# Moving the conversion of the channel weights to a later place in a planned order, with other places set anew

## The chip, the cores and the metric

The kernel runs on one core of a Trainium2 chip. The core has five engines that work beside each other, each through its own instructions in order: TensorE (PE) multiplies matrices, VectorE (DVE) and GpSimd (POOL) work elementwise, ScalarE (ACT) computes functions and copies, and SyncE (SP) issues the transfers between the memory and the core. They wait for each other through semaphores. The metric is the time of one execution in microseconds on the device.

## The reference

A hashed attention feeds a mixing layer. For 4 batches, 8 heads, 768 positions and 64 values per head:

```python
bits = (q @ proj > 0), (k @ proj > 0)            # 6 bits make a bucket
scores = (q @ k.T) / 8, -1e9 where the buckets of query and key differ
x = softmax(scores) @ v                          # heads side by side: (4, 768, 512)
theta = x @ w_theta
y = w_tok_r @ (x * cos(theta)) + w_tok_i @ (x * sin(theta))
u = x + y
out = u + relu(u @ w_ch)
```

w_theta and w_ch are 512 x 512, w_tok_r and w_tok_i 768 x 768; they arrive as 64-bit floats.

## The kernel before

**The work.** Attention goes by batch and pair of heads. For a pair, q and k are loaded and transposed (line 592), split into a high and a low part (597, 600), their sign bits computed (pb, 626), and the operands qt and kt put together by transfers on the SP queue (672 to 681). The maxima of the rows are taken from scores sq (723) and put into qt as a row (747). Then, for chunks of 512 columns, the scores st are multiplied, ACT takes the exponential pf (801) and its half-precision part p (807), POOL the rest of it (813), and PE sums po. norm (862) writes a head's columns of x. V has its own preparation (448 to 525).

The mixing of a batch (function moe) follows when its attention is done, and so runs beside the attention of the next batch. It takes theta for six tiles of 128 positions (transposed 907, hi and lo 912 and 916, product ps_th, then n 948 and the remainder 951), sine and cosine for two groups of three tiles (973, 974), then for each tile and each of the two parts f (985) and its two halves z (990, 996), the token sums py, u (1024), the channel product ps_r with wch, the end (1031) and the store (1034).

**The weights.** Each is turned from 64-bit floats to a high and a low part on the chip, once, before its first use. `widened` (349) loads the raw words on SP (358), builds the 32-bit magnitude with two DVE steps (366, 370), takes the sign and the magnitude on ACT (375, 376) and multiplies them on POOL or DVE (379, 382, 383). `split_weight` (389) adds the high part on ACT (394) and the low part on POOL or DVE (397). w_theta comes in four pieces of 128 x 512, w_ch in eight of 128 x 256. `prep_wtok` (402) does the token weights in T = 6 pieces, and transposes them on PE (424 to 428).

**The order.** Nothing of it is written out. Every operation has a due place, in units of attention: a batch is 24 units, a head 3. Batch b's mixing has G = 24 (b + 1). `issue_all` first walks the list by due place and gives the users of each buffer pool their ranks. Then it plays through the engines with estimated durations: whenever one is free, it takes, of the operations whose inputs are ready, the one due first for which buffers are there, so that an operation may run far ahead of its place where an engine would idle. Two things limit that. A buffer may be taken out of rank only within a window: less than 3 places past the first rank not yet served for the pools m and tmp, otherwise 1. And an operation is held back when one due over 2 units (AHEAD) earlier would become ready within 0.3 of its duration (HOLD). The sequence found is the program: on the chip each engine keeps it.

**The pools that matter here.** tmp has 3 buffers in SBUF; n (948), f (985) with its halves, and both buffers of a w_ch piece (the raw words and the floats) come from it. z0 and z1 have one each; the mixing's z lie in them, and the token weights and w_theta are built in them before. x has 2, for the attention's result, and the raw words of the token weights and of w_theta. m is 4 PSUM banks, for transposes, bits, po, py, theta and channel products.

**The due places.** Places of w_ch are WC + WCS (c + half / 2), lines 1093 and 1094. The token weights stand at W0 + WS tau (1043), w_theta at WTH + WTS c. For batch 0 theta of tile tt has 24 + 0.82 tt, the f of a group 24 + 0.82 (t1 - 0.5), where t1 is 3 and 6, and the token sum of tile t and what follows from it 24 + 8.904 + 2.702 t, with the sums themselves spread over the 6.16 units ahead of that. `at` (302) looks for a value of its own for a batch (TH0_3) and else takes the general one (TH0).

Of the kernel before, what the change touches and what calls it, by code (L numbers as in the profile page):

```python
# [31 lines left out]
def lsh_attention_moe_kernel(ctx: ExitStack, tc: tile.TileContext, q, k, v, proj, w_theta, w_tok_r, w_tok_i, w_ch, aff, out):  # L32
    nc = tc.nc
    PE, ACT, DVE, POOL = nc.tensor, nc.scalar, nc.vector, nc.gpsimd

    B, H, S, D = q.shape
# [17 lines left out]
    def bank(sl, shape, nm):  # L54
        return psum[sl.pool].tile(shape, F32, tag=sl.tag, bufs=1, name=nm)
# [52 lines left out]
    def op(name, prio, alts, deps=(), slots=(), table=None):  # L108
        return Op(name, prio, alts, deps, slots, table)

    def issue_all():
        left = {}
        rng = random.Random(SEED)
        for i, o in enumerate(ops):
# [63 lines left out]
        def key(o, e):  # L178
            return o.key
# [28 lines left out]
        while todo:  # L208
            progress = False
            for e in START:  # L210
# [3 lines left out]
                for o in avail[e]:  # L214
                    k_ = key(o, e)
                    if best is not None and k_ >= best:
                        continue
                    end = now + (HOLD * o.alts[e][0] if e != "SP" else 0)
                    if any(x.at < end and key(x, e)[0] + AHEAD < k_[0] for x in soon[e]):
                        continue  # L220
# [78 lines left out]
    def on(e, dur, fn):  # L299
        return {e: (dur, fn)}  # L300

    def at(nm, b):
        return globals().get(f"{nm}_{b}", globals()[nm])

    def pick(g, rule, alts):
        for lo, hi, engines in rule:
            if lo <= g < hi:
                return {e: alts[e] for e in engines}
        return alts
# [34 lines left out]
    def pow2_scale(amax, inv, s):  # L344
        DVE.tensor_scalar(inv, amax, 1e-30, 2.0**-13, ALU.max, ALU.mult)
        DVE.tensor_scalar(inv.bitcast(U32), inv.bitcast(U32), MASK, None, ALU.bitwise_and)
        DVE.tensor_scalar(s.bitcast(U32), inv.bitcast(U32), MASK, None, ALU.bitwise_xor)
# [39 lines left out]
    wready = {"th": [], "ch": [], "tk": []}  # L387

    def split_weight(src, dst, c, cols, nm, tag, stage, prio, by=1.0):
        lo, n = cols  # L390
        k_ = n / DM
        t, g, sz = widened([src[c * P : (c + 1) * P, lo : lo + n].bitcast(U32)], n, f"{nm}{c}_{lo}", tag, prio, stage=stage, by=by)
        dh, dl = (d[:, c, lo : lo + n] for d in dst)
        h_ = op("wh", prio, on("ACT", 100 + 420 * k_, lambda: ACT.activation(dh, t["w"][:, 0], AF.Copy)), [g], [sz])

        def low(eng):
            return lambda: eng.tensor_tensor(dl, t["w"][:, 0], dh.bitcast(F32), ALU.subtract)

        wready[nm].append(h_)
        wready[nm].append(op("wl", prio, {"POOL": (130 + 1100 * k_, low(POOL)), "DVE": (65 + 535 * k_, low(DVE))}, [h_], [sz]))  # L400

    def prep_wtok(tau, prio):
        am = const.tile([P, 1], F32, name=f"wam_{tau}")
        def scale(t):
            t["s"] = ap_.tile([P, 1], F32, tag="scw", bufs=T, name=f"scw_{tau}")
            pow2_scale(am, sinv[:, tau : tau + 1], t["s"])

        t, g, sz = widened(
            [src.bitcast(U32).rearrange("(p t) s -> p t s", t=T)[:, tau, :] for src in (w_tok_r, w_tok_i)],
            S, f"t{tau}", f"z{tau % 2}", prio, am, scaled=scale,  # L410
        )
        cs = slice(tau * P, (tau + 1) * P)
        TC = 4
        for c0 in range(0, 2 * T, TC):
            def chunk(c0=c0):
                u = {}
                sm_ = Slot("m")
                hi, lo = (wtk_[i].rearrange("p r t s -> p (r t) s")[:, c0 : c0 + TC, cs] for i in range(2))

                def tr():  # L420
                    u["pt"] = bank(sm_, [P, TC, P], f"pwt_{tau}_{c0}")
                    for n in range(TC):
                        r, tt = divmod(c0 + n, T)
                        PE.transpose(u["pt"][:, n, :], t["w"][:, r].rearrange("p (c t) -> p t c", t=T)[:, tt], ident)

                d = op("wtr", prio, on("PE", 109 * TC, tr), [g], [sz, sm_])
                e = op("wth", prio, on("ACT", 55 + 106 * TC, lambda: ACT.activation(hi, u["pt"], AF.Copy)), [d], [sm_])
                wready["tk"].append(op("wtl", prio, on("DVE", 66 + 133.5 * TC, lambda: DVE.tensor_tensor(lo, u["pt"], hi, ALU.subtract)), [e], [sm_]))

            chunk()  # L430
# [6 lines left out]
    vready = {b: [] for b in range(B)}  # L437

    def prep_v(b, hp, prio):
# [86 lines left out]

        r = op("vload", prio + LV0, on("SP", [(450, 2 * S * D * 4)], load), slots=[svb])
        r = op("vamax", prio, on("DVE", 870, amax), [r], [svb])
# [136 lines left out]
    def assemble(j, n_, t, prio, free_after):  # L665
# [12 lines left out]
        def bits():  # L678
# [7 lines left out]
            op("assemble", prio, on("SP", [(1000, 4 * D * n)] * 2 + [(1000, 2 * hd * n)] * 4, parts), t["parts"] + free_after, [sh]),  # L686
            op("assbits", prio + AB, on("SP", [(780, NM * n)] * 2, bits), t["bits"] + free_after, [sr]),
        ]
# [8 lines left out]
    def maxima(h, n_, b, G, asm):  # L697
# [14 lines left out]
        for n, (parts, cs) in enumerate(units):  # L712
            def one(n=n, parts=parts, cs=cs):
# [10 lines left out]

                pr = G + at("MX0", b) + at("MX1", b) * n * T / len(units)
                a = op("qmax", pr, on("PE", 280, scores), asm, [sx])
# [26 lines left out]

        pr = G + at("MX0", b) + at("MX1", b) * T
        a = op("vboth", pr, on("DVE", 110, both), vs, [smc])
# [11 lines left out]
    def step(g, b, h, blk, mxt, vt, piece):  # L767
# [15 lines left out]
        for c in range(nc_):  # L783
            def chunk(c=c):
# [18 lines left out]
                def p1(e):  # L803
                    def go():
                        o_ = wide("p1", sp1, F16)
                        if e == "ACT":
                            ACT.activation(o_, u["pf"], AF.Copy)  # L807
                        else:
                            DVE.tensor_copy(o_, u["pf"])
                    return go  # L810

                def p2(eng):
                    return lambda: eng.tensor_tensor(wide("p2", sp2, F16), u["pf"], u["p1"], ALU.subtract)  # L813
# [20 lines left out]
                last[n_].append(a)  # L834
                i = op("pf", G + PF, on("ACT", 490, pf), [a], [ss, spf], table="exp")
                d = [done] if done else [mxt["ftd"]] + vt["ready"]
                f = [sft] if c == 0 else []
                if vt["full"]:
                    return op("pv4", G + KV, on("PE", 900 + 29 * ni * (c == 0), pv), d + [i], [spf, sm_, vt["slot"], sx] + f)
                k1 = op("p1", G + KA, pick(g, P1, {"ACT": (525, p1("ACT")), "DVE": (337, p1("DVE"))}), [i], [spf, sp1])  # L840
                k2 = op("p2", G + KB, pick(g, P2, {"DVE": (610, p2(DVE)), "POOL": (1090, p2(POOL))}), [k1], [spf, sp1, sp2])
                return op("pv", G + KV, on("PE", 385 + 29 * ni * (c == 0), pv), d + [k1, k2], [sp1, sp2, sm_, vt["slot"], sx] + f)

# [19 lines left out]

        r = op("recip", g + KN, on("DVE", 90, recip), [done], [sm_])
        n = op("norm", g + KN, on("DVE", 135 + 67 * n_, norm), [r], [sm_, sx])
        for i in range(*piece):
# [3 lines left out]
    def moe(b, G):  # L870
        sx = xslot[b]
        sz = [Slot("z0"), Slot("z1")]
        t = {}
# [8 lines left out]
            t["z"] = {(r, i): zt[r][:, :, i] for r in range(2) for i in range(2)}  # L882
            t["zw"] = [zt[r].bitcast(F32).rearrange("p t i d -> p t (i d)") for r in range(2)]

        st0 = op("moe", G, on("DVE", 800, start), wready["tk"] + vready[b], sz)

        cnt = [0]
        tail = TAIL
# [151 lines left out]
    for b in range(B):  # L1040
        xready[b] = [[] for _ in range(NQ)]
    for tau in range(T):
        prep_wtok(tau, W0 + WS * tau)
    for c in range(NC):
        split_weight(w_theta, wth, c, (0, DM), "th", "z0", "x", WTH + WTS * c, 1.0 / TWO_PI)
        for half in range(2):
            split_weight(w_ch, wch, c, (half * DM // 2, DM // 2), "ch", "tmp", "tmp", WC + WCS * (c + 0.5 * half))
    g = 0
    for b in range(B):
        phase = str(b)  # L1050
        for hp in range(NP):
            t = prep_qk(b, hp, g, g)
# [3 lines left out]
            for j in range(2):  # L1056
                n = ((b * NP + hp) * 2 + j) % SETS
                free_after, last[n] = last[n], []
                G = g + sum(BLOCKS[k_][1] // 2 for _, k_ in order[: order.index((j, 0))])
# [5 lines left out]
    for b in range(B):  # L1065
        phase = str(b)
        moe(b, (b + 1) * H * NQ)
# [11 lines left out]
TAIL = ["m", "s"]  # L1079
ORDERS = [[(0, 0), (0, 1), (1, 0), (1, 1)], [(0, 0), (1, 0), (0, 1), (1, 1)]]  # L1080
WIN = {"m": 3, "tmp": 3}
MX0 = -3.0
MX1 = 0.377
PIECES = [{1: (0, 3)}, {0: (0, 2), 1: (2, 3)}]
PF = 0.11
KA = 0.3
KB = 0.629
KV = 0.573
KN = 1.022
AB = 0.145  # L1090
WTH = 16.607
WTS = 1.0
WC = 19.051
WCS = 0.722
P1 = [(0, 999, ["ACT"])]
P2 = [(0, 999, ["POOL"])]
# [1 line left out]
GR1 = 0  # L1098
GROUPS = [[(0, 3), (3, 6)], [(0, 4), (4, 6)], [(0, 2), (2, 4), (4, 6)]]
JIT = 0  # L1100
SEED = 0
TH0_3 = -1.231
TH1_3 = 0.851
Y0_3 = 9.278
# [1 line left out]
Y1_3 = 2.611  # L1106
MX0_0 = -3.0
MX1_0 = 0.377
AS0_0 = -4.85
PV0_0 = -4.074  # L1110
QK0_0 = -6.0
QK1_0 = -5.94
HOLD = 0.3
AHEAD = 2.0
QKL = -8.933
QK0 = -6.006
QK1 = -5.0
AS0 = -2.867
PV0 = -4.114
LV0 = -4.543  # L1120
W0 = 0.4
WS = 3.097
TH0 = 0.0
# [47 lines left out]
```

## Time and profile before

| what | value |
|---|---|
| median of 3 timed runs | 867.27 us (866.17 to 867.66) |
| the profiled execution | 863.75 us |
| its span, from the first to the last instruction | 862.0 us |
| mean granted clock of TensorE | 0.978 |
| instructions of the matrix products with w_ch | from 273.0 us on |
| conversion of w_ch, first to last instruction | 14.5 to 179.9 us |
| conversion of w_theta, first to last instruction | 132.8 to 184.1 us |

Times inside a profile count from the start of its span. An engine's busy time is the time in which it executes; a PE that is shown busy may still run at a lower clock, which stands beside it as the granted clock (1.00 is full speed). The durations that the prediction uses come from this one profiled execution; the timed runs are others, without the profiler.

### The profile page before, as it was taken

The page shows a single profiled execution, that of the slowest core. Times are in us where ns is not written, and L with a number is a line of the kernel's source. Part 1 is how long each engine was busy: PE and PEld are TensorE (multiplying, and loading weights), DVE is VectorE, ACT ScalarE, POOL GpSimd, SP SyncE. Part 2 cuts the span into 40 slices and gives each one's busy share as a digit, 9 for nine tenths or more (in the row PEclk, how much of TensorE's full clock was granted, in tenths as well). Part 3 has the DMA queues.
Part 4 walks back from the last instruction along what each step waited for, and adds up shares of the span by engine and source line. Part 5 has one row for each costly group of instructions (what it writes and reads, how often), then busy time and mean ns, then how long its engine had stood idle before and what let it go on. Part 6 is the DMA issues. An engine that isn't in the chain of part 4 may idle for free.

```text
span 862.0 us, 18152 instructions
## 1 busy us (share of the span) xinstructions
PE 808.4 (94%) x7000; PEld 581.2 (67%) x7000; DVE 555.2 (64%) x976; ACT 531.8 (62%) x917; POOL 462.2 (54%) x500
## 2 busy tenths in 40 slices
PE   5879898799999999999999999999999999998997
PEld 3557676568667766788667766778667766675554
DVE  6998999885776545675685554675785555235522
ACT  3579788787785554477885553577885553657200
POOL 2377788884665452565756452565766452641200
PEclk9979799999999999999999999999999999999999
DMA  9487574851225161453316152443316041000000
GB/s 230 113 255 179 166 206 98 193 131 35 67 48 139 34 130 49 108 125 63 78 27 146 37 123 65 109 114 73 77 36 151 21 94 43 14 13 1 13 25 37
DMA packets 79350, 79.03 MB, mean 92 GB/s; under 512 B 56184, under 2 KB 60472, under 8 KB 79264
## 3 DMA queue, kind: packets, MB, share of 16 engines
q1 hardware_dynamic: 79264, 77.88, 37.1%
q8 instruction: 55, 0.90, 0.4%
q14 instruction: 31, 0.25, 0.1%
HBM read 32.51 MB, written 6.29 MB: 45 GB/s over the span
## 4 chain that ended last, share of the span: by engine, by line
PE 70%; DVE 12%; ACT 11%; POOL 3%; issue 3%; DMA 2%; SPq 0%; ACTq 0%; DVEq 0%; POOLq 0%
PE py L76 20%; PE st L76 13%; PE po L76 10%; PE ps_r L76 8%; PE sq L76 6%; PE ps_th L76 5%; DVE mc L723 3%; PE pb L76 3%; ACT pf L801 2%; POOL p L813 1%; ACT p L807 1%; PE pt L592 1%; PE pt_u L907 1%; DVE hl L600 1%; ACT z L974 1%
## 5 line engine op out<-in xcount | busy, mean ns | idle before, releaser
L813 POOL TENSOR_TENSOR p<-pf,p 128x512 f16<-128x512 f32 x288 | 344.4, 1219 | 230.4 <-ACT p L807 107.7
L801 ACT ACTIVATE pf<-st 128x512 f32<-128x512 f32 x288 | 165.9, 596 | 156.3 <-PE st L76 144.5
L723 DVE TENSOR_REDUCE mc<-sq 128x1 f32<-128x512 f32 (+1 forms) x288 | 191.9, 681 | 48.7 <-PE sq L76 47.4
L76 PE MATMUL py<-z,wtk 128*128 128x512 f16 x864 | 218.3, 383 | 0.5 <-DVE z L996 0.3
L76 PE MATMUL st<-qt,kt 108*128 108x512 f32 (+3 forms) x768 | 196.8, 368 | 10.5 <-ACT pf L801 9.4
L807 ACT ACTIVATE p<-pf 128x512 f16<-128x512 f32 x288 | 172.4, 631 | 9.0 <-PE po L76 6.1
L76 PE MATMUL po<-vv,p 128*128 128x65 f16 (+1 forms) x3456 | 154.6, 195 | 5.2 <-POOL p L813 5.0
L76 PEld LDWEIGHTS <-p 128*128 128x128 f16 x3456 | 133.4, 99 | 36.4 <-issue 17.3
L76 PE MATMUL sq<-kt,qt 108*128 108x256 f32 (+1 forms) x384 | 135.0, 407 | 18.0 <-DVE mc L723 17.3
L76 PEld LDWEIGHTS st<-qt,kt 108*128 108x128 f32 (+1 forms) x768 | 119.9, 193 | 31.1 <-ACT pf L801 18.3
L76 PEld LDWEIGHTS <-wtk 128*128 128x128 f16 x864 | 72.9, 99 | 87.5 <-issue 24.4
L76 PEld LDWEIGHTS sq<-kt,qt 108*128 108x128 f32 x384 | 69.6, 198 | 38.9 <-DVE mc L723 20.1
L996 POOL TENSOR_TENSOR z<-f,z 128x512 f16<-128x512 f32 x40 | 53.0, 1341 | 68.5 <-ACT z L990 58.5
L985 DVE SCALAR_TENSOR_TENSOR f<-x,zsc,z 128x512 f32<-128x512 f32 x48 | 55.4, 1196 | 14.4 <-ACT z L973 12.1
L76 PE MATMUL ps_r<-wch,h_u 128*128 128x512 f32 x192 | 62.5, 407 | 0.7 <-ACT h_u L912 0.7
L76 PE MATMUL ps_th<-wth,h_x 128*128 128x512 f32 x192 | 62.5, 407 | 0.4 <-ACT h_x L912 0.4
L1031 DVE SCALAR_TENSOR_TENSOR x<-ps_r,x 128x512 f32<-128x512 f32 x24 | 16.6, 692 | 67.0 <-PE ps_r L76 67.0
L912 ACT ACTIVATE h_u<-pt_u 128x512 fp32r<-128x512 f32 x24 | 14.3, 597 | 54.0 <-PE pt_u L907 54.0
L600 DVE TENSOR_TENSOR hl<-pt,hl 128x512 fp32r<-128x512 f32 x48 | 32.1, 683 | 22.9 <-ACT hl L597 20.0
L597 ACT ACTIVATE hl<-pt 128x512 fp32r<-128x512 f32 x48 | 28.4, 599 | 26.3 <-PE pt L592 25.9
L76 PEld LDWEIGHTS ps_th<-wth,h_x 128*128 128x128 f32 x192 | 36.0, 191 | 9.5 <-ACT h_x L912 0.6
L76 PEld LDWEIGHTS ps_r<-wch,h_u 128*128 128x128 f32 x192 | 35.1, 188 | 9.3 <-ACT h_u L912 0.9
(130 smaller groups left out, 983.2 us busy)
## 6 DMA issues: line engine op xcount, KB each, us to landing
qt<-hl SPq DMA_DIRECT2D x31, 384.0 KB
kt<-hl SPq DMA_DIRECT2D x31, 384.0 KB
nat<-in_q_dram SPq DMA_DIRECT2D x32, 192.0 KB
nat<-in_k_dram SPq DMA_DIRECT2D x32, 192.0 KB
vb<-in_v_dram SPq DMA_DIRECT2D x16, 384.0 KB
out_dram<-x SPq DMA_DIRECT2D x24, 256.0 KB
qt<-hl SPq DMA_DIRECT2D x62, 96.0 KB
kt<-hl SPq DMA_DIRECT2D x62, 96.0 KB
```

Source lines behind the costliest of these rows:

```text
L76: PE.matmul(out_, l, r, start=start, stop=stop, skip_group_check=True)
L592: PE.transpose(u["pt"][:, ts(n, P)], t["nat", i][:, tt].rearrange("p h d -> p (h d)"), ident)
L597: ACT.activation(hf(0)[:, cs], u["pt"], AF.Copy)
L600: DVE.tensor_tensor(hf(1)[:, cs], u["pt"], hf(0)[:, cs].bitcast(F32), ALU.subtract)
L723: DVE.tensor_reduce(col()[:, cs], u["sq"], AX.X, ALU.max)
L801: ACT.activation(wide("pf", spf, F32), u["st"], AF.Exp, scale=1.0 / math.sqrt(D))
L807: ACT.activation(o_, u["pf"], AF.Copy)
L813: return lambda: eng.tensor_tensor(wide("p2", sp2, F16), u["pf"], u["p1"], ALU.subtract)
L912: ACT.activation(u["hi"], u["pt"], AF.Copy)
L985: DVE.scalar_tensor_tensor(u["f"], tl[b][:, tt], zsc[:, b : b + 1], t["zw"][r][:, tt], ALU.mult, ALU.mult)
L996: return lambda: eng.tensor_tensor(t["z"][r, 1][:, tt], u["f"], t["z"][r, 0][:, tt], ALU.subtract)
L1031: DVE.scalar_tensor_tensor(tl[b][:, to], r_["ps"], 0.0, tl[b][:, to], ALU.max, ALU.add)
```

## The change

The eight pieces of w_ch get due places from 28.159 to 30.69 instead of 19.05 to 21.58, that is, in the second batch's attention (24 to 48) instead of the first's. Other places are set anew with it. The first operation of a batch's mixing is due 0.5 units before its theta instead of at G.

```diff
@@ moe
-        st0 = op("moe", G, on("DVE", 800, start), wready["tk"] + vready[b], sz)
+        st0 = op("moe", G + at("TH0", b) - 0.5, on("DVE", 800, start), wready["tk"] + vready[b], sz)
@@ prep_wtok
-            S, f"t{tau}", f"z{tau % 2}", prio, am, scaled=scale,
+            S, f"t{tau}", "z0" if tau >= LATE else f"z{tau % 2}", prio, am, "z1" if tau >= LATE else "x", scaled=scale,
...
     for tau in range(T):
-        prep_wtok(tau, W0 + WS * tau)
+        prep_wtok(tau, W0 + WS * tau if tau < LATE else WL0 + WLS * (tau - LATE))
...
-MX0 = -3.0
+MX0 = -3.274
...
-PF = 0.11
+PF = 0.16
...
-KV = 0.573
-KN = 1.022
-AB = 0.145
+KV = 0.583
+KN = 0.872
+AB = -0.02
 WTH = 16.607
-WTS = 1.0
-WC = 19.051
+WTS = 1.058
+WC = 28.159
 WCS = 0.722
...
-SEED = 0
+SEED = 162248
...
-AS0_0 = -4.85
+AS0_0 = -5.618
...
-QK0_0 = -6.0
+QK0_0 = -6.17
...
+LATE = 6
+WL0 = 22.0
+WLS = 3.0
+TH0_0 = 0
+TH1_0 = 0.82
+Y0_0 = 8.904
+Y1_0 = 2.702
+YS_0 = 6.16
...
-LV0 = -4.543
+LV0 = -4.311
```

MX0 is where the maxima stand before their head (batch 0 has its own value, which stays), PF, KV and KN are the places of the exponential, of PE's sum and of the norm behind their step, AS0 and QK0 (here with batch 0's own values) those of the assembly of qt and kt and of the transposes before it, AB what the sign rows' transfers come behind the assembly, and LV0 the load of V before its preparation. SEED sets off random shifts of the places, whose size JIT is 0. LATE is compared with tau, which runs from 0 to 5.

## The prediction

> **What bounds the kernel now.** I read the busy line first, then a table by stage, with the stages cut where the chain of work that ended last starts the theta projection of a batch.
>
> ```profile
> span 862.0 us, 18152 instructions
> PE 808.4 (94%) x7000; PEld 581.2 (67%) x7000; DVE 555.2 (64%) x976; ACT 531.8 (62%) x917; POOL 462.2 (54%) x500
> ```
> ```profile
> 197.41 5.61 PE ps_th L76 x24
> ...
> 232.33 2.82 PE ps_th L76 x12
> ...
> 273.14 2.96 PE ps_r L76 x12
> ...
> 393.23 5.61 PE ps_th L76 x24
> ...
> 588.12 5.61 PE ps_th L76 x24
> ```
>
> The chain's columns are start and length. Theta of batches 0, 1 and 2 starts at 197.41, 393.23 and 588.12, so batch 0's attention lasts 197.4 us, and the next two stretches, each an attention plus the channel-mixing work of the batch before, last 195.8 and 194.9. That batch 0 takes as long without any mixing is the oddity to explain.
>
> ```profile
> 0.00:35.00 35.00, 22.70 (x73) 15.23 (x74) 28.17 (x70) 14.37 (x21) 9.80 (x22) 1.00 0.70 177
> 35.00:140.00 105.00, 89.33 (x886) 70.36 (x886) 96.85 (x164) 84.93 (x153) 76.67 (x79) 0.89 0.72 191
> 140.00:160.00 20.00, 18.62 (x225) 15.30 (x224) 20.00 (x34) 17.18 (x34) 17.41 (x15) 1.00 0.59 136
> 160.00:180.00 20.00, 14.00 (x140) 9.96 (x138) 15.75 (x31) 14.44 (x30) 17.19 (x21) 0.83 0.64 166
> 180.00:197.40 17.40, 16.08 (x216) 13.06 (x214) 14.28 (x30) 15.77 (x30) 16.05 (x14) 1.00 0.52 115
> 197.40:240.00 42.60, 40.55 (x299) 30.39 (x297) 27.12 (x46) 32.22 (x49) 22.20 (x25) 0.96 0.18 41
> 240.00:275.00 35.00, 34.74 (x323) 23.63 (x322) 25.59 (x41) 25.64 (x45) 26.42 (x29) 1.00 0.41 89
> 275.00:393.20 118.20, 117.30 (x1116) 85.63 (x1115) 68.49 (x127) 64.73 (x118) 58.92 (x66) 1.00 0.42 99
> 393.20:588.10 194.90, 192.46 (x1734) 139.30 (x1733) 121.20 (x214) 122.30 (x211) 107.56 (x119) 0.99 0.37 85
> ```
>
> Columns: stretch, length, then busy time of PE, PE weight load, DVE, ACT and POOL, the granted clock, DMA. From 197.4 on PE is idle 3.2 us in 195.8 (2.05 + 0.26 + 0.90) and 2.4 in 194.9: there TensorE is the bound, and DVE is 62% busy. Before that it is the other way round: DVE fills 96.85 of 105 us and then 20.00 of 20, while PE idles 15.7 us of the 105 at a clock of 0.89. Between 160 and 180 neither fills; PE idles 6.0 us there and the clock falls to 0.83. So 14 us of DVE work cost something in the first batch and should be cheap in the second.
>
> **The change part by part.** *Removed from batch 0:* the eight pieces of w_ch. The same table for the tile wf_ch alone (DVE, ACT, POOL):
>
> ```profile
> 0.00:35.00 35.00, 0.69 (x2) 1.67 (x4) 1.46 (x2) 1.00 0.70 177
> 35.00:140.00 105.00, 5.31 (x8) 4.56 (x11) 5.38 (x6) 0.89 0.72 191
> 140.00:160.00 20.00, 4.06 (x4) 0.40 (x1) 0.00 (x0) 1.00 0.59 136
> 160.00:180.00 20.00, 3.89 (x7) 3.23 (x8) 3.79 (x3) 0.83 0.64 166
> ...
> sum 862.00, DVE 13.95 ACT 9.87 POOL 10.63; mean DVE 1.27 ACT 0.90 POOL 0.97
> ```
>
> 35 to 140: DVE is 92% busy, so its 5.31 us come back nearly one for one; 4.5. 140 to 160: DVE is full and 4.06 us go, but POOL is free only 2.6 of these 20 us and then is the limit; 2.6. 160 to 180: the stall. POOL loses 3.79 us of its 17.19, DVE 3.89 of 15.75; PE idles 6.0, the most that can be won at the same clock; 3.5. Before 35 the work (0.69 us of DVE) fills waits; 0. Sum **10.6 us**. Bounds: all DVE time counted at its worth (5.31 x 105/96.85 = 5.8, 4.1, and 6.0 in the stall) gives 15.9; nothing at all if another engine's wait takes each place.
>
> The port is a second effect. In the first batch a residual on POOL takes longer than its usual value, from the groups of the window 0 to 197.4 and the summary of line 813:
>
> ```profile
> L813 POOL TENSOR_TENSOR p<-pf,p 128x512 f16<-128x512 f32 x76 | 99.5, 1333 | 22.9 <-ACT p L807 16.6 <-PE pt L592 2.4 <-PE st L76 0.9
> ```
> ```profile
> L813 POOL TENSOR_TENSOR p<-pf,p x288: 1147/1165/2953, 36.9 to 770.8; 128x512 f16<-128x512 f32 x144
> ```
> ```profile
> L985 DVE SCALAR_TENSOR_TENSOR f<-x,zsc,z x48: 737/1070/1656, 216.0 to 803.7; 128x512 f32<-128x512 f32 x48
> ```
>
> 76 times (1333 - 1165) ns are 12.8 us of POOL. Part of that goes with w_ch's DVE work; I count nothing extra, since the sum above lets DVE time come back in full. The Trainium skill, page SBUF — State Buffer, section "Who interferes with whom", says that a VectorE and a GpSimd instruction which need the port pair they share exclude each other for a whole instruction, and that the order of issue decides who waits. The stretched residuals agree. By that rule the change brings the conflict along: f (line 985), between 737 and 1656 ns now, would wait for w_ch's POOL steps in batch 1, which nothing in this trace can show.
>
> *Added to batch 1.* Due 28.159 to 30.69, behind batch 0's theta (due 24 to 28.1, the last at 232.33) and ahead of the first channel projection (due 33.1, at 273.14). Each piece takes two of the three tmp buffers, and ranks let a buffer user start at most two places ahead of its turn. In rank order come the six n and the first three tiles' six f, then piece 0, the other six f, and pieces 1 to 7. So piece 0 borrows two buffers around 235 to 245, just when f of the second group wants three, and the other seven come after these f. The last of those f ends with z at 251.4 + 1.2:
>
> ```profile
> L996 POOL TENSOR_TENSOR z<-f,z x8: 1157/1207/1606, 224.0 to 251.4; 128x512 f16<-128x512 f32 x8
> L985 DVE SCALAR_TENSOR_TENSOR f<-x,zsc,z x8: 741/1350/1650, 224.6 to 248.8; 128x512 f32<-128x512 f32 x8
> ```
>
> The last piece of before shows the pace of one (its load on the SP queue, then DVE):
>
> ```profile
> 171.47 0.37 SPq L358 DMA_DIRECT2D w_ch<-in_moe_w_ch_dram  x1
> ```
> ```profile
> 174.26 0.88 DVE L366 TENSOR_SCALAR wf_ch<-w_ch 128x256 uint32<-128x256 uint32 x1 [1.49 <-DMA w_ch<-in_moe_w_ch_dram]
> ...
> 175.55 0.89 DVE L370 SCALAR_TENSOR_TENSOR wf_ch<-w_ch,wf_ch 128x256 uint32<-128x256 uint32 x1
> ...
> 179.48 0.41 DVE L397 TENSOR_TENSOR wch<-wf_ch,wch 128x256 fp32r<-128x256 f32 x1
> ```
>
> Issue to end of the raw data's use is 5.0 us (171.47 to 176.4), to the very end 8.4. Seven in a row from 252.6: 35 + 3.4 gives 291 on the old time axis; with DVE and landing undisturbed some 3.6 us each, about 281. Either way the first channel projection, at 273.1, is **8 to 18 us late**. TensorE loses nothing by that if the order holds other work for it meanwhile. From the page's groups:
>
> ```profile
> L76 PE MATMUL py<-z,wtk 128*128 128x512 f16 x864 | 218.3, 383 | 0.5 <-DVE z L996 0.3 <-POOL z L996 0.2
> L76 PE MATMUL st<-qt,kt 108*128 108x512 f32 (+3 forms) x768 | 196.8, 368 | 10.5 <-ACT pf L801 9.4
> ...
> L76 PE MATMUL po<-vv,p 128*128 128x65 f16 (+1 forms) x3456 | 154.6, 195 | 5.2 <-POOL p L813 5.0
> ...
> L76 PE MATMUL sq<-kt,qt 108*128 108x256 f32 (+1 forms) x384 | 135.0, 407 | 18.0 <-DVE mc L723 17.3
> ```
>
> The attention of one of the 32 heads is (196.8 + 154.6 + 135.0) / 32 = 15.2 us, and the token sums are 218.3 / 24 = 9.1 us for each of the 24 tiles, of which the next two may start early. Some 15 to 33 us of cover stand against 8 to 18. I take 0 for the projection. On SP's queue the eight loads cost 0.4 us each, but one that waits for buffers holds up the rows of maxima behind it, which the next head's scores need: 1 us of the 3.2 issued. Piece 0 holds its first buffer 5.0 us, by which f and z can come late while TensorE has other work: between 0 and 5.0, nearer to 0 because PE idles only 0.26 us in 240 to 275; 2. Together **3 us**. Bounds: 0, and 18 + 5 + 3.2 = 26 if no cover holds. Once past, DVE has 68.49 of 118.20 us filled: 14 us fit.
>
> *Dues set anew.* Maxima of batches 1 to 3 0.274 earlier, norms 0.15 earlier, V loads 0.23 later, the first batch's assembly 0.77 earlier, the sign rows' transfers just ahead of the assembly's instead of behind: no row prices them. Equal stretches already differ by 0.9 us (195.8, 194.9), the most to be won is PE's 2.4 us idle in a batch, and as much could be lost; I take 0, ends -4 and +4. LATE equals the number of tiles (6), the _0 values repeat the general ones and JIT is 0, so these select nothing; the earlier start operation waits for z, which the batch before still holds; 0.
>
> **Sum:** -10.6 + 3 = -7.6 us. The profiled execution took 863.75 us around its span of 862.0, which gives 856.2; the three timed runs have a median of 867.27, 3.5 above. I forecast for these: **859.7 us**.
>
> **Rivals.**
> 1. *Slower: the channel projection blocks TensorE.* PSUM bank users of the pool m also go in rank order, at most two past an unfilled turn. If py of two tiles and po hold the four banks when ps_r's turn comes, PE finds nothing else for up to 18 us. Then -10.6 + 3 + 17 = +9.4, 876.7 us; it ends slower than before once more than 7.6 us are uncovered. For it: the pieces must run one by one through three buffers. Against: 15.2 us of attention whose bank is given by then. 18%. The Trainium skill, page TensorE: Matmul & The Clock Gate, section "Part 1: The HAM clock gate (the "warmup" mystery)", has the clock halve after about 3.4 us of idling; in this trace a hole of 3.95 us in 165 to 170 is followed by 0.50 in the next row. By that rule a hole of rival 1 costs some 2 us more.
>
> ```profile
> 165.00:170.00 5.00, 1.05 (x14) 0.91 (x15) 4.03 (x9) 2.60 (x6) 5.00 (x4) 0.82 0.94 200
> 170.00:175.00 5.00, 4.99 (x35) 3.08 (x33) 2.04 (x3) 3.37 (x8) 4.72 (x7) 0.50 0.41 88
> ```
>
> 2. *Given back.* w_theta's four pieces and the token weights stay where they are; if POOL and these in-order waits keep batch 0's pace, only some 3 us (of the 4.06 in the stretch where DVE is full) are won and batch 1 takes them: 867.3. With it the case that the work doesn't move at all (3%; against it: its buffers rank behind theta's). 12%.
> 3. *More:* PE also regains its clock of 0.89 and batch 1 hides all: -15, 852. 7%.
>
> **How the numbers follow.** Forecast of 3 to 13 us faster 57%, a smaller gain of 2 to 3 us 6%, rival 3 7%: faster 0.70. Rival 2: same 0.12. Rival 1: slower 0.18. About 0.2% (1.7 us) is what a measurement of this kernel tells from no change. The range goes from rival 3's 852 to 871, which leaves out the worse half of rival 1; the likeliest case alone is 854 to 864.
>
> **What would show it.** Theta of batch 0 starts near 187 instead of 197.4; DVE still above 90% up to 130; the hole at 165 is gone or smaller. The eight w_ch loads lie between 225 and 280, and from theta to the first ps_r it is 84 us or more instead of 75.7 (273.14 - 197.41). Theta to theta in batch 1 is 196 to 199. I am wrong if batch 0 ends later than 194, or if batch 1 has PE idle over 8 us.

## The result, and the profile after

The changed kernel takes 853.6 us (four runs, 849.53 to 854.34) against 867.0 (866.17 to 867.66): a ratio of 0.9843, with a 95% interval of 0.9823 to 0.9862. The forecast was 859.7, in a range of 852 to 871. The profiled executions lie closer together, 854.34 and 863.75, so that of the 13.4 us between the medians the two profiles show 9.4. The rest is spread from run to run: the changed kernel's profile is the slowest of its four runs.

The chain of the changed kernel that ended last (start, length) shows where these 9.4 us lie:

```profile
190.14 5.70 PE ps_th L76 x24
...
288.16 2.80 PE ps_r L76 x12
...
383.84 5.61 PE ps_th L76 x24
...
576.80 5.63 PE ps_th L76 x24
```

Theta of batch 0 starts 7.3 us earlier (197.41 to 190.14). The next two stretches are 193.7 and 193.0 us instead of 195.8 and 194.9, and what follows 576.80 takes 275.8 us of the span instead of 273.9. The sum: 7.3 + 2.1 + 1.9 - 1.9 = 9.4. The first channel product stands 98.0 us behind theta, 22 us further than before's 75.7.

By stages, with the same columns as before (PE, PE weight load, DVE, ACT, POOL, granted clock, DMA):

```profile
0.00:35.00 35.00, 21.10 (x63) 14.03 (x64) 27.27 (x67) 12.51 (x16) 8.32 (x20) 0.67 0.69 171
35.00:130.00 95.00, 80.44 (x890) 63.43 (x888) 89.08 (x152) 78.37 (x133) 71.97 (x72) 0.99 0.72 189
130.00:160.00 30.00, 28.13 (x278) 21.82 (x277) 27.17 (x50) 25.75 (x52) 19.68 (x22) 0.92 0.54 136
160.00:190.10 30.10, 27.34 (x300) 22.01 (x301) 20.50 (x40) 22.88 (x45) 25.38 (x24) 0.83 0.60 140
190.10:240.00 49.90, 48.16 (x353) 34.60 (x352) 37.29 (x59) 41.87 (x67) 27.11 (x30) 1.00 0.18 41
240.00:290.00 50.00, 49.97 (x487) 34.10 (x486) 40.35 (x75) 30.72 (x65) 34.61 (x39) 1.00 0.44 112
...
383.80:576.80 193.00, 190.73 (x1734) 139.36 (x1733) 119.00 (x214) 121.56 (x212) 107.25 (x119) 1.00 0.37 86
```

The kernel before in the second of these stretches:

```profile
35.00:130.00 95.00, 81.30 (x806) 64.36 (x806) 88.50 (x151) 76.46 (x135) 68.48 (x71) 0.87 0.73 196
```

Two things are to be seen. DVE is no emptier between 35 and 130: 89.08 of 95 us is 94%, where before it was 93% with the w_ch pieces in it. The heads are further on in that time, with 890 instructions on PE instead of 806. And TensorE is full while those pieces are converted (49.97 of 50.00 between 240 and 290), although the projection that needs them waits. The pieces themselves, from the summary of their tile, lie where the forecast had them:

```profile
L366 DVE TENSOR_SCALAR wf_ch<-w_ch x8: 281/290/645, 223.4 to 284.7; 128x256 uint32<-128x256 uint32 x8
L370 DVE SCALAR_TENSOR_TENSOR wf_ch<-w_ch,wf_ch x8: 426/550/1270, 223.8 to 285.0; 128x256 uint32<-128x256 uint32 x8
```

### The profile page after: what moved, and what is told of

It reads as the page before. It is cut to its first block, busy times and chain, and to the rows that moved or that the text cites. A ratio compares the mean times of both kernels' runs of the same rounds, so it can differ in the third digit from the quotient of the medians.

```text
span 852.6 us, 18177 instructions
## 1 busy us (share of the span) xinstructions
PE 803.6 (94%) x7000; PEld 580.1 (68%) x7000; DVE 550.2 (65%) x982; ACT 528.5 (62%) x917; POOL 455.1 (53%) x494
## 4 chain that ended last, share of the span: by engine, by line
PE 69%; DVE 13%; ACT 11%; issue 3%; POOL 2%; DMA 2%; SPq 0%; ACTq 0%; DVEq 0%; POOLq 0%
PE py L76 19%; PE st L76 12%; PE po L76 10%; PE ps_r L76 8%; PE sq L76 6%; PE ps_th L76 6%; DVE mc L723 4%; PE pb L76 3%; ACT pf L801 2%; PE pt L592 2%; ACT p L807 2%; PE pt_u L907 1%; DVE f L985 1%; DVE wf_t L379 1%; DVE hl L600 1%
## 5 line engine op out<-in xcount | busy, mean ns | idle before, releaser
L76 PE MATMUL st<-qt,kt 108*128 108x512 f32 (+3 forms) x768 | 194.4, 368 | 9.0 <-ACT pf L801 8.1
L76 PEld LDWEIGHTS <-p 128*128 128x128 f16 x3456 | 130.8, 98 | 37.3 <-issue 17.9
L76 PE MATMUL sq<-kt,qt 108*128 108x256 f32 (+1 forms) x384 | 131.3, 403 | 14.6 <-DVE mc L723 11.6
L996 POOL TENSOR_TENSOR z<-f,z 128x512 f16<-128x512 f32 x38 | 51.0, 1355 | 66.0 <-ACT z L990 53.9
L985 DVE SCALAR_TENSOR_TENSOR f<-x,zsc,z 128x512 f32<-128x512 f32 x48 | 53.6, 1156 | 7.1 <-ACT z L973 4.8
L1024 DVE SCALAR_TENSOR_TENSOR x<-py,sw,x 128x512 f32<-128x512 f32 x24 | 18.0, 750 | 41.8 <-PE py L76 41.8
```

The source lines that it names most:

```text
L76: PE.matmul(out_, l, r, start=start, stop=stop, skip_group_check=True)
L985: DVE.scalar_tensor_tensor(u["f"], tl[b][:, tt], zsc[:, b : b + 1], t["zw"][r][:, tt], ALU.mult, ALU.mult)
L996: return lambda: eng.tensor_tensor(t["z"][r, 1][:, tt], u["f"], t["z"][r, 0][:, tt], ALU.subtract)
L1024: DVE.scalar_tensor_tensor(tl[b][:, to], res["py"], t["sw"][:, to : to + 1], tl[b][:, to], ALU.mult, ALU.add)
```

## The experiments

Each was compared with the kernel before on the same chip. "Theta" is the start of batch 0's first theta product in the profile.

| run | time, us | ratio (95% interval) | theta |
|---|---|---|---|
| kernel before | 866.0 to 867.0 (medians) | 1 | 197.4 |
| changed kernel | 853.6 | 0.9843 (0.9823 to 0.9862) | 190.1 |
| e1, WC alone | 866.5 | 1.0004 (0.9977 to 1.003) | 195.6 |
| e2, all but WC | 872.0 | 1.0068 (1.0042 to 1.0094) | 204.8 |
| e3, before without w_ch work | 865.0 | 0.9980 (0.9954 to 1.0006) | 194.3 |
| e4, changed without w_ch work | 850.6 | 0.9826 (0.9794 to 0.9859) | 188.1 |
| e5, WC, AS0_0, QK0_0 | 864.5 | 0.9977 (0.996 to 0.9995) | 195.0 |
| e6, changed, AS0_0 and QK0_0 back | 853.4 | 0.9856 (0.9829 to 0.9883) | 191.8 |
| e7, changed, shuffled | 895.7 | 1.0343 (1.0307 to 1.0378) | 195.4 |
| e8, before, shuffled | 913.5 | 1.0553 (1.0529 to 1.0577) | 206.8 |
| e9, changed, AB back | 861.1 | 0.9939 (0.9908 to 0.997) | 197.4 |
| e10, changed, MX0 back | 852.2 | 0.9843 (0.9819 to 0.9867) | 188.2 |
| e11, WC and AB | 857.7 | 0.9900 (0.9874 to 0.9925) | 190.5 |
| e12, AB alone | 871.8 | 1.0066 (1.004 to 1.0092) | 203.6 |

**Is it the move of w_ch?**

```diff
-WC = 19.051
+WC = 28.159
```

> The kernel before with one number changed: WC = 28.159 instead of 19.051, every other due place as before. My theory (the move of w_ch itself brings the gain, the other places little): theta of batch 0 starts 6 to 8 us earlier than before's 197.4, batch 1 costs up to 2 us, the time is 5 to 9 us below the kernel before (about 860). Rival (the places set anew bring it, the move alone opens a hole): theta of batch 0 may start earlier, but batch 1 grows by more than 5 us and the time is within 3 us of before or above it.

It isn't, not by itself. Theta starts 1.8 us earlier, batch 1 is 197.6 us long instead of 195.8, and the time is that of the kernel before. The opposite edit, in the changed kernel:

```diff
-WC = 28.159
+WC = 19.051
```

> The changed kernel with WC put back to 19.051, so that only the other places are new. My theory: without the move these bring at most 4 us (863 to 867). Rival: they bring most of it (857 or less), batches 1 and 2 being 2 us shorter each as in the changed kernel, batch 0 too.

Neither expectation held: with the new places and w_ch in the first batch, the kernel is slower than before, and theta 7.4 us later. The two together say that the move and some of the other places act only jointly.

**What is the work worth where it stands?** Here the loop over `split_weight(w_ch, ...)` is left out and wch set to constants:

```diff
+    for i, w_ in enumerate(wch):
+        POOL.memset(w_.bitcast(F32), (0.03, 1e-5)[i])
...
-        for half in range(2):
-            split_weight(w_ch, wch, c, (half * DM // 2, DM // 2), "ch", "tmp", "tmp", WC + WCS * (c + 0.5 * half))
```

> The kernel before with the eight loads and conversions of w_ch left out (wch is filled with a constant once, at the start). Shows what this work costs where it stood. My theory, from the prediction's 10.6 us: theta of batch 0 starts at 185 to 190 and the time is 8 to 12 us below before. Rival (other waits take its place): 3 us or less. An edit that takes the work out without moving it is also free of what it does in batch 1.

> The changed kernel with the same work left out. Shows what it costs where it stands now. My theory: theta of batch 0 stays near 190, and the whole is 0 to 3 us below the changed kernel (850 to 854), although its first channel projection comes some 15 us earlier. Rival (the late projection costs and something else made up for it): 5 us or more below the changed kernel, at the place where PE waits between 240 and 300.

The first is the blow to the forecast's main step. Taking all of the 13.95 us of DVE, 9.87 of ACT and 10.63 of POOL out of the first batch of the kernel before gains 0.2%, with an interval that reaches past no change, where 10.6 us (1.2%) were worked out. In the profile theta comes 3.1 us earlier, and what follows it is 2.8 us longer. The whole first batch, before and then without w_ch:

```profile
0.00:197.40 197.40, 160.74 (x1527) 123.92 (x1528) 175.05 (x324) 146.69 (x265) 137.12 (x149) 0.92 0.68 174
```
```profile
0.00:194.30 194.30, 157.13 (x1521) 122.05 (x1522) 166.81 (x307) 137.56 (x239) 118.53 (x135) 0.94 0.64 165
```

DVE is busy 8.2 us less, not 13.95, and idles 5.1 us more; only 3.1 us of it shorten the batch. In the fullest part, without w_ch:

```profile
35.00:80.00 45.00, 35.57 (x319) 27.73 (x317) 39.79 (x65) 33.28 (x56) 23.36 (x26) 0.92 0.72 201
80.00:120.00 40.00, 35.41 (x405) 28.93 (x402) 35.10 (x59) 31.84 (x56) 28.04 (x29) 0.87 0.71 188
120.00:160.00 40.00, 35.98 (x383) 28.77 (x383) 36.91 (x65) 31.68 (x61) 27.25 (x29) 0.91 0.50 123
```

Between 35 and 160 DVE is busy 111.8 of 125 us without w_ch, and 116.85 in the kernel before: of w_ch's 9.4 us there, about half stays filled. By the tiles, no conversion comes ahead of theta that stood behind it before. But the order now gives DVE three of w_theta's products (383) and two more of its low parts (397) that POOL did before, and w_theta's DVE steps take 12.9 us instead of 9.5. The second run puts the price of w_ch in its new place at 3.0 us (853.6 to 850.6), the intervals overlapping; the forecast took 3. The two profiles differ by 5.0 us: 2.0 ahead of theta, where neither kernel has work of w_ch, 1.6 in batch 1, and the rest behind batch 2.

**Is it the first batch's operands?** The new AS0_0 and QK0_0 were the nearest suspect, since they touch the first batch alone.

```diff
 WC = 28.159
-AS0_0 = -4.85
+AS0_0 = -5.618
-QK0_0 = -6.0
+QK0_0 = -6.17
```

> The kernel before with three numbers changed: WC = 28.159, AS0_0 = -5.618, QK0_0 = -6.17; that is the move of w_ch and the earlier transposes and operand assembly of the first batch. Theory A (the first batch is paced by when the next head's operands are there; the work of w_ch had kept them from being made earlier, so both edits are needed): theta of batch 0 starts at 188 to 192, and the time is 857 to 861, what is left being batches 1 and 2. Theory B (the gain lies in the places for all batches, KN, KV, PF, AB, LV0): theta at 195 or later, 864 to 868.

> The changed kernel with AS0_0 and QK0_0 put back, the complement of the last. Theory A: theta of batch 0 at 194 to 198, batches 1 and 2 still 193 to 194 long, 859 to 863. Theory B: theta at 188 to 192, the time within 2 us of the changed kernel.

Theory A falls by both: with these places and the move there is next to nothing (0.9977), and without them nothing is missing (853.4). Theory B, that the cause is in the places for all batches, stays.

**How much does any order matter?**

```diff
-JIT = 0
+JIT = 0.03
-SEED = 0
+SEED = 1
```

> The changed kernel with JIT = 0.03 and SEED = 1: every due place shifted at random by up to 0.03 units (0.25 us), which means nothing by itself. Theories A and B both have causes that such a shift leaves alone: 852 to 857. Theory C (the time depends on the order found as a whole, and the changed kernel's is a lucky one): it loses 5 us or more.

> The kernel before with the same random shift. Theories A and B: 864 to 870, like before. Theory C: anywhere between 855 and 880, and the distance from before measures what a meaningless change of order is worth.

Both lose far more than the change is worth, 42 and 47 us, and most of it in the later batches: in the first of the two, theta of batch 0 is only 5.3 us later. So a shift of 0.25 us at most isn't neutral. As the code reads, it gives operations due at the same place, such as the steps of one tile, different places; that this is what costs is not shown. The shift can't serve as a measure of chance, as I had meant it to, but it shows that the time hangs on the order itself, while the work is the same. Theory C, that the changed kernel's order is a lucky one as a whole, is neither borne out nor excluded.

**Which place is it?** Put back singly in the changed kernel, KN and LV0 leave the order of the instructions on all five engines as it is, and KV and the start operation change it in few places. AB, MX0, PF and WTS each make it a new one from early on; AB and MX0 were run.

```diff
-AB = -0.02
+AB = 0.145
```

> The changed kernel with AB put back to 0.145, so that a head's sign rows go to SP behind the row of maxima of another head again instead of ahead of its assembly. Theory D (the sign rows' place on the SP queue paces the first batch: in the kernel before they left 2.5 to 3.6 us after the last assembly transfer where the row came between, in 3 of the 7 assemblies before 175 us): theta of batch 0 at 194 to 198, batches 1 and 2 within 1 us of the changed kernel's 193.7 and 193.0, the time 857 to 862. Theory E (the earlier maxima, MX0, bring the gain in all batches): within 2 us of the changed kernel.

```diff
-MX0 = -3.274
+MX0 = -3.0
```

> The changed kernel with MX0 put back to -3.0 (batch 0 has its own value and keeps its maxima). Theory D: theta of batch 0 stays at 189 to 192; batches 1 and 2 go back to 195 to 196, since MX0 is what shortened them; 855 to 859. Theory E: 860 or more, batch 0 no better than 195 where it overlaps the next batch's maxima. If neither moves by over 2 us, MX0 is without weight.

```diff
-AB = 0.145
+AB = -0.02
-WC = 19.051
+WC = 28.159
```

> The kernel before with two numbers changed: WC = 28.159 and AB = -0.02. Theory D: these two alone bring the gain of the first batch: theta at 189 to 192, the time 856 to 861, batches 1 and 2 still 195 to 196. Theory E: like WC alone (866.5), theta at 195.

> The kernel before with one number changed: AB = -0.02; w_ch stays in the first batch. It fills the table of the two numbers (neither 866, WC alone 866.5, both 857.7). Theory D1 (the sign rows' place and the weights' work are separate waits on one path, and only without both is the first batch faster): 864 to 872, theta of batch 0 at 194 or later. Theory D2 (AB is what counts, w_ch is hidden wherever it stands): 856 to 860, theta at 189 to 192.

The times are those that theory D gives in the form D1. Without AB the changed kernel has theta at 197.4 again and 861.1 us; MX0 has no weight for the whole (it shortens batch 2 from 194.9 to 193.0 and what follows is longer by as much). The two numbers alone make this table of medians:

| | AB = 0.145 | AB = -0.02 |
|---|---|---|
| WC = 19.051 | 866 to 867 | 871.8 |
| WC = 28.159 | 866.5 | 857.7 |

One edit does nothing, the other loses 5 us, and both together win 8 to 9. Some expectations missed beside that. Batch 1 was to keep the changed kernel's 193.7 us without AB and measured 195.8 (e9); it was to keep 195 to 196 with both edits alone and measured 193.6 (e11). So the pair acts in batch 1 too. (The expectation for AB speaks of a lag of 2.5 to 3.6 us in 3 of 7 assemblies; read more closely, the three cases are 3.6, 3.6 and 3.9, of nine.)

**What AB does** to the order can be read on the SP queue; what of it brings the time is less plain. First the kernel before (start and length of the issue):

```profile
53.84 0.59 SPq L676 DMA_DIRECT2D kt<-hl  x1
54.53 0.78 SPq L747 DMA_DIRECT2D qt<-row  x1
55.41 1.45 SPq L752 DMA_DIRECT2D ft<-fl  x2
56.96 0.39 SPq L450 DMA_DIRECT2D vb<-in_v_dram  x1
57.41 0.77 SPq L680 DMA_DIRECT2D qt<-rows  x1
58.23 0.74 SPq L681 DMA_DIRECT2D kt<-rows  x1
```

The sign rows (680, 681) are the last part of a head's operands, and here they leave 3.6 us after the last transfer of the assembly, behind the row and flags of another head and a load of V. With both edits (e11) the rows of a pair's second head go ahead of its assembly:

```profile
83.83 0.76 SPq L680 DMA_DIRECT2D qt<-rows  x1
84.63 0.72 SPq L681 DMA_DIRECT2D kt<-rows  x1
85.46 0.71 SPq L747 DMA_DIRECT2D qt<-row  x1
...
87.80 0.70 SPq L672 DMA_DIRECT2D qt<-hl  x1
...
93.81 0.59 SPq L676 DMA_DIRECT2D kt<-hl  x1
```

Theory D has the late rows pace the first batch. The trace doesn't bear that out for their own head. Counted in the order of the program, the assembly above is head 3's, and the first product that uses it, an sq, starts at 67.51, 8.5 us after its rows have left; for head 5, the next such case, it is 7.9 us. (The one such transfer on the chain, issued at 82.86, took 3.9 us.) What waits visibly is the row of maxima of head 1 (747). DVE had it ready at 48.8, and it left at 54.53, behind the six transfers of head 3's assembly:

```profile
48.55 0.27 DVE L740 TENSOR_SCALAR row<-pmx 6x128 fp32r<-6x128 f32 x1
...
58.44 3.69 PE L76 MATMUL st<-qt,kt 108*128 108x512 f32 x8
...
67.51 0.40 PE L76 MATMUL sq<-kt,qt 108*128 108x512 f32 x1
```

With AB that row goes ahead of the assembly: ready at 48.2, sent at 48.95, head 1's first st at 52.88 instead of 58.44 (e11). But e12, which loses, has the same (49.2, 49.75, 54.20). The two part later: in e12 the rows of heads 3, 5 and 7 wait 4.7, 4.6 and 5.3 us on the queue, in e11 0.3, 5.4 and 0.0. From heads 1 to 7 such waits add up to 13.4 us before, 10.7 in e1, 15.3 in e12, 6.9 in e11 and 5.4 in the changed kernel; but in e2, whose theta comes later than in any of these, it is 7.9. They are a part of the account at most, and no run changes them alone.

The heads' pace differs as the theta does. Ends of the eight norms of batch 0 (line 862):

| run | heads 0 to 7, us |
|---|---|
| before | 58.5, 82.1, 101.7, 123.9, 143.1, 157.9, 181.1, 194.7 |
| e1, WC | 61.1, 83.4, 105.7, 120.5, 143.2, 160.5, 180.6, 192.8 |
| e12, AB | 60.8, 83.8, 101.4, 127.1, 147.1, 165.0, 185.8, 200.8 |
| e11, both | 61.5, 79.6, 96.9, 115.0, 132.1, 155.6, 173.3, 187.9 |
| changed | 61.0, 77.2, 95.1, 111.6, 129.8, 152.8, 174.3, 187.5 |

With both edits heads 1 to 4 take 16 to 18 us each; with one, or none, 15 to 26. At head 4, e11 is 11.0 us ahead of before (132.1 to 143.1). **Where AB alone loses** shows first in e12's fourth head, 25.7 us long; behind it e12 is 3.2 us later than before, at the last norm 6.1. The chain in that stretch:

```profile
97.63 6.85 DMA w_t<-in_moe_w_tok_i_dram
...
107.26 1.28 DVE wf_t L366
...
109.40 2.48 DVE wf_t L370
...
112.33 5.46 DMA w_t<-in_moe_w_tok_i_dram
```

And by pieces of 5 us:

```profile
90.00:95.00 5.00, 3.36 (x42) 2.56 (x41) 5.00 (x7) 2.70 (x5) 5.00 (x5) 0.67 0.95 200
95.00:100.00 5.00, 3.70 (x19) 2.35 (x20) 4.93 (x10) 2.19 (x4) 3.27 (x4) 0.50 0.54 140
100.00:105.00 5.00, 4.70 (x46) 4.14 (x45) 4.90 (x8) 3.76 (x7) 2.33 (x2) 0.81 0.89 323
105.00:110.00 5.00, 3.04 (x17) 2.26 (x16) 3.78 (x5) 4.65 (x9) 2.47 (x3) 0.88 0.07 27
```

The chain goes through two late loads of token weights and their conversion on a DVE that is full from 90 to 105, and ACT converts a piece of w_ch in between (at 106.5 and 107.8). PE is busy 3.0 to 4.7 us of 5 at a clock of 0.50 to 0.88. This is read, not tested: which of the steps between the two edits makes the hole, no run takes out by itself. A late load alone doesn't tell the runs apart, for the chain of the faster e11 holds one of 7.88 us at 81.29. PF, WTS, KV and the start operation were not tried singly either; they hold the remaining 4 us between e11 and the changed kernel, or some of it.

## Why the prediction was right, and where it was not

**The direction and the time** were right, the reason only in part. The range of 852 to 871 holds 853.6, near its lower end. That is partly luck: the gain counted for the move alone is not there (e1, e3), and one of similar size came from a term put at 0.

**"14 us of DVE work cost something in the first batch and should be cheap in the second."** The second half held: w_ch costs about 3.0 us where it stands now. The first half is the step that failed. The 10.6 us were worked out from DVE being 92% busy, as if each microsecond taken from it came back. Without the work the first batch of the kernel before is 3.1 us shorter and the whole 0.2% (e3); with the work moved, 1.8 us and nothing (e1). So DVE's fill was not the bound that it was taken for: most of what was freed became DVE's idle time or was filled again. What did bound the first batch stays open. The traces show waits in the order of the SP queue and at the loads of the token weights, and no run isolates either.

**"Dues set anew ... I take 0, ends -4 and +4."** This term held the gain: with w_ch moved, all of these dues together are worth -12.9 us (e1 to the changed kernel), far outside the ends, and with w_ch in the old place +5 (e2). AB, named there as the sign rows' transfers just ahead of the assembly's, is worth -7.5 us in the changed kernel (e9), +5 alone and -8.8 with the move (e1 to e11). I bounded the term by PE's idle time in the later batches (2.4 us). From e1 to the changed kernel 5.5 us lie in the first batch, which that bound left out and where PE was idle 15.7 us in one stretch alone, and 3.9 and 2.0 in batches 1 and 2.

**The parts summed:** -10.6 for batch 0 measured -7.3, though by another way; +3 for batch 1 measured -2.1 in length, and batch 2 gained 1.9, for which I had nothing. In these two the clock is a part: the stretch from 197.4 to 240 ran at 0.96 before, that from 190.1 to 240 at 1.00 now, and batch 2 at 0.99 and 1.00.

**Rival 1**, the late projection: its mechanism occurred, its price didn't. The product came 22 us later, even beyond the 8 to 18 forecast, and PE idled 0.03 us between 240 and 290, because the cover (attention and token sums) was there. **Rival 2** described the outcome of the move alone well (e1), and had 12%. **Rival 3**, a gain of 15 from the clock as well, is near the measured one, and its mechanism is not settled. In the profiled run the clock was worse at the start (0.67 in the first 35 us, with PE busy 21.1 of them) and better from 35 to 130 (0.99 against 0.87), where PE did 84 instructions more in about the same busy time; over the whole first batch it was 0.89 against 0.92. Of the four runs this one has the lowest mean clock, 0.971. The other three have 0.983 to 0.988, where 54 runs of the kernel before lie between 0.956 and 0.982, with a mean of 0.971. An estimate from these: 0.015 of 860 us are up to 13 us of TensorE's time. Whether the clock is a cause of the shorter time or follows from fewer holes, no run tells.

**The port.** The residuals on POOL, stretched to 1333 ns in the first batch, were expected to shorten with w_ch gone. In the changed kernel they didn't, in e3 by a third of the stretch (the groups of the windows 0 to 190.1 and 0 to 194.3; line 813 is 815 in e3):

```profile
L813 POOL TENSOR_TENSOR p<-pf,p 128x512 f16<-128x512 f32 x76 | 99.5, 1331 | 41.4 <-ACT p L807 34.0 <-PE st L76 3.7 <-issue 1.8
```
```profile
L815 POOL TENSOR_TENSOR p<-pf,p 128x512 f16<-128x512 f32 x76 | 95.4, 1274 | 51.9 <-ACT p L809 48.1 <-PE st L76 1.6 <-issue 1.3
```

The rule itself (the Trainium skill, SBUF — State Buffer, "Who interferes with whom") isn't touched by that. The long residuals stand beside the token weights' steps of 128 x 1536 (370 and 379), which all these kernels run: the nine that run mostly beside such a step take 2.24 us on average before and 2.18 in the changed kernel. Of some 14 us above 1.15 us each they make up 9.9 before; those that ran mostly beside a step of w_ch make up 1.0.

**The signs named beforehand.** DVE above 90% up to 130: yes, but so it was in runs without any gain. Theta near 187: 190.1, and earlier than 194. The w_ch loads between 225 and 280: from 219.0 to 279.6. Batch 1 of 196 to 199: 193.7. **The hole at 165** became smaller, but another one opened, at the last load of the token weights:

```profile
115.98 8.63 DMA w_t<-in_moe_w_tok_i_dram
```
```profile
120.00:125.00 5.00, 3.55 (x49) 2.62 (x50) 4.66 (x13) 2.20 (x4) 4.74 (x10) 1.00 0.94 246
125.00:130.00 5.00, 1.57 (x15) 0.79 (x13) 5.00 (x7) 2.74 (x3) 1.78 (x3) 0.81 0.53 119
130.00:135.00 5.00, 5.00 (x17) 3.49 (x17) 4.83 (x10) 3.46 (x10) 0.89 (x1) 0.51 0.62 187
```

ACT's next instruction in order is the sign of that weight, and the exponentials behind it wait; PE is busy 1.57 of 5 us and is then granted half its clock. That a hole halves the clock agrees with the Trainium skill (TensorE: Matmul & The Clock Gate, "Part 1: The HAM clock gate (the "warmup" mystery)"). Head 5, which follows, takes 23 us where those before it took 16 to 18; that is one place where the first batch may still have something to give.

## What to carry to other kernels

In an order that is filled greedily and made anew by every edit, a busy engine doesn't promise its time back: here 13.95 us taken from an engine 92% busy shortened the batch by 3.1. Before counting on the time that a removed step gives back, look for the instruction of the slow stretch that is late, and for what its queue issues ahead of it. When a change sets many numbers, the small ones can carry it, and two of them may count only together; a table of both with neither and each alone settles that, where undoing one at a time would have credited either with everything. Order among transfers on one queue deserves the same care as order among instructions: here a small row, ready, waited 5.7 us behind a large assembly. And a theory that fits the times has still to be held against the trace: the late rows of theory D had left 8.5 us before their head first used them.

## What the runs showed of the hardware

The same program varies from run to run with the granted clock: ten runs of e1 go from 861.64 us at a mean clock of 0.982 to 870.51 at 0.966 and 870.39 at 0.957, with a correlation of -0.88 between time and clock, and ten of e3 from 858.7 at 0.984 to 868.8 at 0.966 (-0.72). The kernel before, in the same call, spreads from 862.58 to 869.78 in 20 runs (-0.26). Four runs of e4 with clocks of 0.986 to 0.988 lie within 3 us. A difference under 0.5% between two such kernels therefore needs a good many runs; whether a hole costs its own length or also the slower clock behind it, these means can't tell apart.

In the lines above an issue on the SP queue took 0.4 to 0.8 us, and a transfer that was ready waited behind those ahead of it (5.7 us for the row of head 1). A load of token weights stood on the chain for 5.5 to 8.6 us.
